# A new front for an attention + MLP kernel: first quads loaded in halves, log sums by scan, one first-layer group parked in SBUF

## The chip, the cores and the metric

One core of one Trainium2 chip runs one program. The metric is the device time of one execution in microseconds. A core has five engines with a queue each, and every engine works through its queue in order: TensorE (PE; its weight loads are shown apart as PEld), VectorE (DVE), ScalarE (ACT), GpSimd (POOL) and SyncE (SP). DMAs are issued from the queues of SP, ACT and POOL and moved by 16 DMA engines that all of them share. A DMA that also casts (fp32 in memory to bf16 on chip) is issued by GpSimd in this kernel.

## What is computed

Attention with a forget gate for 8 batches x 8 heads, 576 tokens, 64 columns a head; its output, 4608 tokens x 512, goes through an MLP of two layers.

```python
scores = scale * np.matmul(q, k.transpose(0, 1, 3, 2))
cum = np.cumsum(np.log(np.clip(f, 0.0001, 1.0)), axis=-1)
decay = cum[:, :, :, None] - cum[:, :, None, :]
scores = np.where(causal, -1000000000.0, scores + decay)
attn = softmax(scores)
x = (attn @ v).transpose(0, 2, 1, 3).reshape(B * S, H * D)   # 4608 x 512
out = gelu_tanh(x @ w_in) @ w_out                            # 512 -> 2048 -> 512
```

The factor exp(-cum) of the decay is put on the values and on the column that sums the denominators, so that a row's own factor drops out: `wT = exp(-cum - 64)`, `vw = v * wT`, and the denominator is a product with `wT` in bf16 (`w_bf`).

## The kernel before

**Units of work.** Four heads make a quad, 16 quads in all, two to a batch. A quad's scores are written in tiles of `[128 keys, 2 heads, up to 512 queries]` in PSUM (pool `psS`, two buffers), and ScalarE's exp takes them to `pt` in SBUF, which frees the buffer (`scores`, L259). Masks are put on `pt` by GpSimd (`mask`, L287) or by VectorE as a product (`mask_by_product`, L311). `denominators` (L356) multiplies `pt` by `w_bf` on TensorE; VectorE transposes the result, takes reciprocals and spreads them (`rb`). `attn_out` (L374) multiplies `pt` by half of `vw`, and VectorE scales by `rb` into `xT`, the input of the MLP, in a ring of four batches. Chunks of 512 tokens then go through the first layer (`mlp_in`, for chunk 0 in halves of 256 tokens by `mlp_in_half`, L408) with ScalarE's Gelu into `gT`, and through the second (`mlp_out`, L658, for chunk 0; `seven_products` later).

**The order** is written by hand. With `manual_schedule` the instructions of each engine stand in the order in which the code issues them, and a table of words sets that order (`run`, L807): each word names an entry of `ops` (L754) with its numbers. In the words of the tables, `LK.i`/`LQ.i` load k/q of quad i with a cast (L206), `TK.i`/`TQ.i` transpose them on VectorE (L212), `S.i.r` or `H.i.r.g` are scores of round r (for all four heads, or for pair g), `M`/`m` masks on GpSimd/VectorE, `VW`/`vw` the product v * wT on GpSimd/VectorE, `CL` a copy of a part of vw, `D` denominators, `V`/`v` attention output, `J.h.g` a first-layer group of 4 x 128 columns for half h of chunk 0 (`j`: the same in the PSUM buffer of pool `psO`, its Gelu issued later by `GJ`), `F.0.n`/`f.0.n` n steps of the second layer of chunk 0, `WI`/`WO` parts of w_in/w_out, `LP`/`LC`/`LV` parts of v, `X` ScalarE's table for exp, and `B.n.c` n products of c columns on zeros that keep TensorE busy. Quads 0 and 1 have four rounds, whose first covers the first 256 queries, so that D and V of them go in two parts (`D.0.0`, `V.0.0.0`).

**The front** is `setup` (L677) and the first rows of `FRONT` (L75) up to `F.0.4`. `setup` loads f by SyncE, and k and q of quads 0 and 1 whole by GpSimd; VectorE clips f, ScalarE takes the log, TensorE transposes it (L700), ScalarE copies it to SBUF (L702, L703). `CW` (`make_w`, L717) then sums along the tokens on TensorE by products with a triangle of ones and with ones, in fp32 (L719, L721), and ScalarE's exp makes `wT` (L724); `W` casts it (L748). Scores of quad 0 (`S.0.0`) stand between. GpSimd's queue has, behind one another, loads, five memsets (`Z`, L705), masks and `VW`. GpSimd's loads use eight semaphores in turn, so a ninth waits for the first to land.

## Time and profile before

| | |
|---|---|
| runs, us | 324.0 (median), 323.05, 324.26 |
| the profiled execution, us | 323.22 |
| its span, us | 321.4 |
| bytes read from and written to HBM | 36.85 and 9.44 MB |
| first scores (L277) start, us from the span's start | 8.62 |
| first first-layer product (L419) | 21.57 |
| first second-layer product of chunk 0 (L667) | 40.82 |
| first first-layer product of chunk 1 (L395) | 66.25 |

The times in the lower rows are from the chain that ended last. The profile is that of one execution; its span leaves out what lies ahead of the first instruction and behind the last, and the difference to the execution's time is 1.8 us. In the profile's lines, `L277` is line 277 of the kernel before; a line reads engine, operation, output<-input, shapes, and then busy time and mean duration, or start and length. TensorE's instructions overlap in its pipeline, so that a mean duration is longer than the distance from one to the next.

### The profile page before, as it was taken

The page shows a single profiled execution, that of the slowest core. Times are in us where ns is not written, and L with a number is a line of the kernel's source. Part 1 is how long each engine was busy: PE and PEld are TensorE (multiplying, and loading weights), DVE is VectorE, ACT ScalarE, POOL GpSimd, SP SyncE. Part 2 cuts the span into 40 slices and gives each one's busy share as a digit, 9 for nine tenths or more (in the row PEclk, how much of TensorE's full clock was granted, in tenths as well). Part 3 has the DMA queues.
Part 4 walks back from the last instruction along what each step waited for, and adds up shares of the span by engine and source line. Part 5 has one row for each costly group of instructions (what it writes and reads, how often), then busy time and mean ns, then how long its engine had stood idle before and what let it go on. Part 6 is the DMA issues. An engine that isn't in the chain of part 4 may idle for free.

```text
span 321.4 us, 11820 instructions
## 1 busy us (share of the span) xinstructions
PE 309.6 (96%) x5339; PEld 220.7 (69%) x5339; DVE 242.0 (75%) x374; ACT 212.7 (66%) x242; POOL 107.8 (34%) x145
## 2 busy tenths in 40 slices
PE   0899999999999999999999999999999999999996
PEld 0557844544776567776788878767776786688785
DVE  4765337898979879779877987699876866597674
ACT  4676576775766776878767866787586744836610
POOL 8989343522301416400851075205610140000000
PEclk9999999999999999999999999999999999999999
DMA  7999999585126931593139411971011111010203
GB/s 126 218 210 208 247 213 199 104 155 109 35 43 129 227 78 37 116 209 72 39 82 228 87 39 35 190 172 36 7 47 53 37 34 37 30 37 0 100 33 99
DMA packets 47490, 33.41 MB, mean 104 GB/s; under 512 B 29776, under 2 KB 42192, under 8 KB 47440
## 3 DMA queue, kind: packets, MB, share of 16 engines
q0 software_dynamic: 9632, 15.99, 28.3%
q1 hardware_dynamic: 37664, 16.60, 19.1%
q8 instruction: 41, 0.67, 0.9%
q14 instruction: 9, 0.07, 0.1%
q10 hardware_dynamic: 144, 0.07, 0.1%
HBM read 36.85 MB, written 9.44 MB: 144 GB/s over the span
## 4 chain that ended last, share of the span: by engine, by line
PE 91%; ACT 3%; DVE 3%; DMA 2%; issue 1%; POOL 0%; DVEq 0%; POOLq 0%
PE ps_w L600 30%; PE ps_h L395 19%; PE ps_s L277 9%; PE po L347 9%; PE ps_q L520 8%; PE pso L667 4%; PE ps_h L419 4%; PE ps_u L468 4%; DMA q_c<-in_q_dram 2%; PE po_m L333 1%; ACT pt L285 1%; ACT gT L403 1%; DVE xT L379 1%; PE idle_ps L256 1%; PE cum_ps L721 1%
## 5 line engine op out<-in xcount | busy, mean ns | idle before, releaser
L285 ACT ACTIVATE pt<-ps_s 128x1024 bf16<-128x1024 f32 (+2 forms) x100 | 94.0, 990 | 38.6 <-PE ps_s L277 35.9
L291 POOL TENSOR_SCALAR_AFFINE_SELECT pt<-pt 128x512 bf16<-128x512 bf16 (+3 forms) x65 | 41.4, 647 | 95.2 <-ACT pt L285 72.3
L395 PE MATMUL ps_h<-xT,w_in_sb 128*128 128x512 bf16 (+1 forms) x320 | 66.8, 358 | 0.3 <-ACT gT L403 0.2
L395 PEld LDWEIGHTS <-w_in_sb 128*128 128x128 bf16 x320 | 31.2, 98 | 26.6 <-issue 0.6
L600 PEld LDWEIGHTS <-gT 128*32 128x32 bf16 (+1 forms) x1216 | 44.1, 97 | 5.5 <-issue 2.2
L403 ACT ACTIVATE gT<-ps_h 128x1024 bf16<-128x1024 f32 x34 | 34.6, 1017 | 18.7 <-PE ps_h L395 18.4
L600 PE MATMUL ps_w<-w_out_sb,gT 128*32 128x256 bf16 (+1 forms) x1008 | 42.6, 273 | 0.0
L277 PE MATMUL ps_s<-qT,kT 32*128 32x64 bf16 (+5 forms) x896 | 36.3, 263 | 3.2 <-DVE qT L214 3.0
L600 PEld LDWEIGHTS <-gsum 128*32 128x32 bf16 (+1 forms) x948 | 35.4, 97 | 3.8 <-issue 1.5
L231 POOL TENSOR_TENSOR vw<-v_nat,wT 128x1280 bf16<-128x1280 f32 (+1 forms) x13 | 29.6, 2279 | 11.7 <-DMA v_nat<-in_v_dram 11.4
L536 DVE TENSOR_TENSOR usnap<-ps_q,usnap 128x1024 f32<-128x1024 f32 x15 | 17.9, 1222 | 18.6 <-PE ps_q L520 13.2
L277 PEld LDWEIGHTS <-kT 32*128 32x128 bf16 x896 | 16.5, 93 | 19.6 <-issue 10.1
L600 PE MATMUL ps_w<-usum,gsum 128*32 128x256 bf16 (+1 forms) x791 | 30.0, 273 | 0.0
L617 DVE COPY snap<-ps_w 128x512 f32<-128x512 f32 x32 | 21.8, 681 | 6.2 <-PE ps_w L600 6.0
L531 ACT ACTIVATE gT<-usnap 128x1024 bf16<-128x1024 f32 x15 | 15.8, 1054 | 12.1 <-DVE usnap L536 11.8
L379 DVE TENSOR_TENSOR xT<-po,rb 128x576 bf16<-128x576 f32 x26 | 19.5, 752 | 5.6 <-PE po L347 5.3
L347 PE MATMUL po<-pt,vw 128*32 128x64 bf16 (+4 forms) x624 | 22.4, 278 | 0.0
L214 DVE STREAM_TRANSPOSE qT<-q_c 128x576 f32<-128x576 f32 x16 | 19.8, 1246 | 1.7 <-DMA q_c<-in_q_dram 1.7
L347 PEld LDWEIGHTS <-vw 128*32 128x32 bf16 x672 | 14.6, 97 | 9.4 <-issue 2.8
L214 DVE STREAM_TRANSPOSE kT<-k_c 128x576 f32<-128x576 f32 x16 | 19.5, 1246 | 1.9 <-DMA k_c<-in_k_dram 1.9
L208 POOL DMA_DIRECT2D k_c<-in_k_dram x16 | 9.1, 568 | 33.6 <-DVE kT L214 18.0
L520 PEld LDWEIGHTS <-w_in_sb 128*128 128x128 bf16 x160 | 15.6, 98 | 2.5 <-issue 0.4
(135 smaller groups left out, 478.5 us busy)
## 6 DMA issues: line engine op xcount, KB each, us to landing
out_dram<-o_st SPq DMA_DIRECT2D x35, 256.0 KB, 2.3
k_c<-in_k_dram POOLq DMA_DIRECT2D x16, 288.0 KB, 5.3
q_c<-in_q_dram POOLq DMA_DIRECT2D x16, 288.0 KB, 6.3
v_nat<-in_v_dram SPq DMA_DIRECT2D x16, 256.0 KB, 5.4
v_nat<-in_v_dram SPq DMA_DIRECT2D x20, 128.0 KB, 5.1
v_nat<-in_v_dram POOLq DMA_DIRECT2D x8, 256.0 KB, 8.1
w_in_sb<-in_moe_w_in_dram POOLq DMA_DIRECT2D x8, 256.0 KB, 7.8
w_out_sb<-in_moe_w_out_dram POOLq DMA_DIRECT2D x4, 512.0 KB, 11.3
```

The lines of the kernel that those rows point to most:

```text
L214: return nc.vector.transpose(out=dst.rearrange("p s c -> p (s c)").bitcast(FP32) .rearrange("p (t a) -> p a t", a=S // 32), in_=src.rearra ...
L231: return eng.tensor_mul(vw[i % 2][:, t0:t1], vb[:, t0:t1, h0:h0 + 4, :], wT[:, i, t0:t1, :].unsqueeze(3).to_broadcast([128, t1 - t0, 4, D]))
L277: nc.tensor.matmul(tiles[h // 2][:, h % 2, c0:c0 + nq], key_columns(i, key, h, c), qq[32 * h:32 * h + 32, q0:q0 + nq, c], start=(c == 0 an ...
L285: nc.scalar.activation(p[:, 2 * g:2 * g + 2, off:off + n], t[:, :, 0:n], AF.Exp, scale=scale)
L291: nc.gpsimd.affine_select(out=x, in_=x, compare_op=ALU.is_ge, fill=0.0, base=0, pattern=pattern, channel_multiplier=-1)
L347: nc.tensor.matmul(po[r0:r0 + w.shape[-1], 448 + q0:448 + q0 + nq], w, p[:, h, col:col + nq], start=(key in (0, "low")), stop=(key in ("lo ...
L379: nc.vector.tensor_mul(xT[:, 2 * u + x, r0 + s0:r0 + s1], po, rbs[i, part])
L395: nc.tensor.matmul(ph[:, j, n * cols:(n + 1) * cols], w_in_sb[:, dt, 128 * ft:128 * ft + 128], xT[:, dt, h0:h0 + cols], start=(dt == 0 and ...
L403: nc.scalar.activation(gelus(c, 2 * pr, 2), ph, AF.Gelu_apprx_tanh)
L520: nc.tensor.matmul(ps[:, k, HC * n:HC * n + HC], w[:, d, 128 * n:128 * n + 128], x[:, d, :], start=(first and n == 0 and d == 0), stop=(d ...
L600: nc.tensor.matmul(ps[c0:c0 + width, n, cols[0]:cols[1]], x[:, j, 128 * n + c0:128 * n + c0 + width], w[:, j, cols[0]:cols[1]], start=(fir ...
L617: copy(kept[name], ps)
```

## The change

Only the front of the table, the functions that it calls and a few words behind it change.

- k and q of quad 0 come in two parts. The first 256 tokens are loaded by SyncE in fp32 into a part of `pt[1]` that is not in use yet, and cast on chip: k by VectorE (`CK`), q by ScalarE (`CA`). The other 320 tokens, and both parts of quad 1, are loaded by GpSimd with the cast; transposes go by part. f is loaded from ScalarE's queue. ScalarE loads one table that has both log and exp.
- The log sums are made by VectorE's scan along the tokens (`SC`) and then transposed by TensorE (`CT`), in place of the copies and the products L719 and L721. `wT` is made for quads 0 and 1 first (`CE.0`), then for the rest (`CE.1`); the cast likewise (`w.0` on ScalarE, `W.1` on VectorE).
- The memsets of `Z` go from GpSimd to VectorE; that of `logfT` is gone.
- The first-layer groups can be issued in parts (`J.h.g.n`). Group J.0.0 is copied raw to SBUF (`RJ`, into a buffer that is free until later), which frees its PSUM buffer for J.0.1; both have their Gelu later.
- `mlp_out` works on two tiles of 128 tokens in turn, a quarter of the depth at a time, so that w_out's last quarter is needed later.
- The table's front is written anew. Fillers are B.1.512 x3 and B.1.256 x2, where they were B.1.384, B.1.512, B.2.512 x2, B.2.256 and B.1.256 x2. The order of loads is another: all of w_in, then w_out's first part, quad 2's k and q, the rest of w_out, and batch 1's v (`LC`) after quad 3's k and q for the most part. Behind the front, `CL.2` and `CL.3` go to ScalarE (`cl`), `vw.2` stands ahead of `TQ.4` on VectorE, `LV.2.0` comes later, and `VW.3` on GpSimd stands behind `LK.6` and ahead of `M.3.2`, where it stood ahead of `LK.4`.

```diff
+    first = pt[1].rearrange("p h n -> p (h n)").bitcast(FP32)
+    first = [first[:, QA * D // 32 * n:QA * D // 32 * (n + 1)] for n in range(2)]
+
+    def load_first(src, eng, n):
+        eng.dma_start(out=first[n], in_=src[0, 0:4, 0:QA].rearrange("h (p a) d -> h p (a d)", p=32))
+
+    def cast_first(dst, eng, n):
+        copy = eng.copy if eng is nc.scalar else eng.tensor_copy
+        copy(dst[0][:, 0:QA // 32, :].rearrange("p a d -> p (a d)"), first[n])
...
+        if part is not None:
+            s0, s1 = parts[part]
+            return nc.gpsimd.dma_start(
+                out=dst[i % 2][:, s0 // 32:s1 // 32, :].rearrange("p a d -> p (a d)"),
+                in_=src[b, h0:h0 + 4, s0:s1].rearrange("h (p a) d -> h p (a d)", p=32))
...
+    def keep_raw(half, g, copy):
+        raw = (u1, u2, u4)[len(raws)].rearrange("p f n -> p (f n)").bitcast(FP32).rearrange("p (b n) -> p b n", n=QA)
+        raws.append(raw)
+        copy(raw, held[half, g][0])
+        held[half, g][0] = raw
...
-        for n in range(CH // 128):
...
+        for pair in range(CH // 256):
+            psos = [psM.tile([128, D_MODEL], FP32, name="pso", tag="m") for _ in range(2)]
+            for part in range(4):
+                for n in range(2):
...
     def setup():
-        nc.sync.dma_start(out=f_sb, in_=f.rearrange("b h s -> (b h) s"))
-        dmas["LK.0"] = load_one(k, k_c, 0)
-        dmas["LQ.0"] = load_one(q, q_c, 0)
+        load_first(k, nc.sync, 0)
+        nc.scalar.dma_start(out=f_sb, in_=f.rearrange("b h s -> (b h) s"))
+        load_first(q, nc.sync, 1)
+        nc.scalar.preload_act_table_set("natural_log_exp_and_others")
+        load_one(k, k_c, 1, 0)
+        load_one(q, q_c, 1, 0)
         make_identity(nc, ident_f32)
-        dmas["LK.1"] = load_one(k, k_c, 1)
-        dmas["LQ.1"] = load_one(q, q_c, 1)
-        make_upper_triangular(nc, utri_f32, val=1.0, diag=True)
...
+        load_one(k, k_c, 0, 1)
+        load_one(q, q_c, 0, 1)
...
+    def running_sums():
+        nc.vector.tensor_tensor_scan(f_sb, ones_f32[0:BH, 0:1].to_broadcast([BH, S]), f_sb, 0.0,
+                                     op0=ALU.mult, op1=ALU.add)
...
-    def make_w():
-        cum_ps = psM.tile([128, NT * BH], FP32, name="cum_ps", tag="m")
-        nc.tensor.matmul(cum_ps, utri_f32, logfT, start=True, stop=True)
-        for n in range(NT - 1, 0, -1):
-            nc.tensor.matmul(cum_ps[:, n * BH:], ones_f32, logfT[:, :(NT - n) * BH], start=False, stop=True,
-                             skip_group_check=True)
+    def cum_tiles():
+        cums.append(psM.tile([128, NT * BH], FP32, name="cum_ps", tag="m"))
+        for t in range(NT):
+            n = min(128, S - 128 * t)
+            nc.tensor.transpose(cums[0][:n, t * BH:(t + 1) * BH], f_sb[:, 128 * t:128 * t + n], ident_f32)
```

The table's front after the change, with line breaks put in:

```
CK TK.0.0 CA TQ.0.0 LK.1.1 LQ.1.1 LP.0 LP.1 S.0.0 SC TK.1.0 TQ.1.0 CT CE.0 w.0 S.1.0 UT CE.1 M.0.0 WI.0 B.1.512
TK.0.1 TQ.0.1 TK.1.1 H.0.1.0 D.0.0 H.0.1.1 B.1.512 WI.1 M.1.0 TQ.1.1 vw.0.0 vw.1.0 H.0.2.0 B.1.512 H.0.2.1 B.1.256
H.1.1.0 V.0.0.0 V.0.1.0 LP.2 LP.3 WI.2 WI.3 H.1.1.1 D.1.0 H.1.2.0 B.1.256 V.1.0.0 H.1.2.1 V.1.1.0 LP.4 WI.4 WI.5 M.0.1
H.0.3.0 j.0.0.8 H.0.3.1 j.0.0.8 WI.6 M.0.3 H.1.3.0 RJ.0.0 vw.0.1 WI.7 D.0.1 j.0.1.8 H.1.3.1 V.0.0.1 V.0.1.1 j.0.1.8
WO.0 M.1.1 M.1.3 VW.1.1 LK.2 LQ.2 WO.1 GJ.0.0 GJ.0.1 WO.2 D.1.1 J.0.2 WO.3 V.1.0.1 V.1.1.1 LC.1.4 W.1 TR J.0.3 LK.3 LQ.3
LC.1.2 LC.1.0 LC.1.1 J.1.0 LC.1.3 J.1.1 TK.2 J.1.2 TQ.2 LQ.4 J.1.3 LK.4 F.0.4 X F.0.4 S.2.0 F.0.11 TK.3 S.2.2 F.0.6 TQ.3
F.0.4 LK.5 S.2.1 F.0.3 F.0.6 vw.2 TQ.4 m.2.1 S.3.0 cl.2 M.2.2 f.0.5 M.2.0 f.0.2 D.2 S.3.1 LV.2.0 f.0.7 LQ.5 V.2.0 m.3.0
S.3.2 TK.4 LK.6 VW.3 f.0.1 f.0.3 V.2.1 M.3.2 f.0.2 S.4.1 cl.3 m.3.1 LQ.6 f.0.5 TQ.5 H.4.2.1 D.3 H.4.0.1
```

More of the change, by code (lines that the diff above doesn't have):

```diff
@@ L414, in mlp_in_half @@
         n0 = QA * half
+        at = [ph.rearrange("p a (b n) -> p (a b) n", n=QA)]
+        later[half, g] = lambda: nc.scalar.activation(gT[:, 4 * g:4 * g + 4, n0:n0 + QA], at[0], AF.Gelu_apprx_tanh)
+        held[half, g] = at
         for dts in (range(N_DT - 1), range(N_DT - 1, N_DT)):
@@ L425, in mlp_in_half @@
                     )
-        later[half, g] = lambda: nc.scalar.activation(gT[:, 4 * g:4 * g + 4, n0:n0 + QA],
-                             ph.rearrange("p a (b n) -> p (a b) n", n=QA), AF.Gelu_apprx_tanh)
-        if not spare:
-            later[half, g]()
+                    if not spare and j == 3 and dt == N_DT - 1:
+                        later[half, g]()
+                    yield
     def x_block(c, b, t):
```

129 lines of the change are left out of this document (63 added, 66 removed).

## Prediction

> **What bounds the kernel now.** I read the page's busy times first, then those by stretch, then the chain that ended last in order of time. Busy us of each engine, with its share of the span of 321.4 us:
>
> ```profile
> PE 309.6 (96%) x5339; PEld 220.7 (69%) x5339; DVE 242.0 (75%) x374; ACT 212.7 (66%) x242; POOL 107.8 (34%) x145
> ```
>
> TensorE (PE) is busy 309.6 of 321.4 us, so 11.8 us at most can come from filling its gaps; more comes only from giving it less work. The view by stretches cuts the span at the first scores (8.62), the first product of the first layer (21.57), the first product of the second layer (40.82) and the first product of chunk 1 (66.25). Behind each stretch stand the busy us of PE, PEld, DVE, ACT and POOL, the clock, the DMA share and GB/s:
>
> ```profile
> 0.00:8.62 8.62, 0.77 (x6) 0.65 (x7) 4.22 (x14) 3.72 (x5) 7.28 (x20) 1.00 0.76 132
> 8.62:21.57 12.95, 12.68 (x165) 6.95 (x165) 9.08 (x18) 10.23 (x14) 12.35 (x18) 1.00 1.12 217
> 21.57:40.82 19.25, 19.08 (x265) 15.48 (x266) 8.19 (x16) 11.38 (x13) 12.03 (x17) 1.00 1.20 226
> 40.82:66.25 25.43, 25.34 (x454) 12.04 (x453) 17.52 (x25) 18.86 (x21) 12.20 (x16) 1.00 0.81 161
> 66.25:321.40 255.15, 251.72 (x4452) 185.56 (x4451) 203.02 (x304) 168.46 (x191) 63.98 (x77) 1.00 0.36 82
> ```
>
> Of the idle 11.8 us, 7.85 lie ahead of the first scores. From 8.62 to 66.25 PE is idle for 0.53 us, and later for 3.4 us in 255. So a shift of the front passes nearly whole to the end, and so does a new wait of PE. The DMA share, over 1 from 8.62 to 40.82, says that the loads run without a gap: they can be put in another order, hardly all moved forward.
>
> The chain in order of time (start, length, what) has the pieces that the change touches:
>
> ```profile
> 2.03 5.25 DMA q_c<-in_q_dram
> 7.28 0.02 issue
> 7.30 1.27 DVE qT L214
> 8.57 0.04 issue
> 8.62 0.83 PE ps_s L277 x14
> 9.45 0.43 PE idle_ps L256
> 9.88 1.07 PE cum_ps L719 x2
> 10.94 1.66 PE cum_ps L721 x8
> ...
> 40.82 1.73 PE pso L667 x8
> ```
>
> **Part 1: the first scores.** They wait for quad 0's q, which lands at 7.28, and for its transpose. New: SyncE loads 256 of the 576 tokens of k, then of q, 256 KB each; VectorE casts k, ScalarE casts q behind its Ln, and VectorE transposes 8/18 of the words. The DMA issues on SyncE's queue, KB each and median us from issue to landing:
>
> ```profile
> out_dram<-o_st SPq DMA_DIRECT2D x35, 256.0 KB, 2.3
> ...
> f_all<-in_f_dram SPq DMA_DIRECT2D x1, 144.0 KB, 2.7
> out_dram<-v_nat SPq DMA_DIRECT2D x1, 128.0 KB, 1.9
> ```
>
> The timeline (start, length): SyncE's first issue,
>
> ```profile
> 0.82 0.58 SPq L678 DMA_DIRECT2D f_all<-in_f_dram  x1
> ```
>
> VectorE's clip of f, with its wait for the load,
>
> ```profile
> 3.58 0.45 DVE L694 TENSOR_SCALAR f_all<-f_all 64x576 f32<-64x576 f32 x1 [1.32 <-DMA f_all<-in_f_dram]
> ```
>
> ScalarE's Ln,
>
> ```profile
> 4.06 0.68 ACT L695 ACTIVATE f_all<-f_all 64x576 f32<-64x576 f32 x1 [1.97 <-DVE f_all L694]
> ```
>
> and PE's five transposes of it:
>
> ```profile
> 4.89 0.77 PE L700 MATMUL ps_lt<-ident_f,f_all 64*128 64x64 f32 x5 [4.89 <-ACT f_all L695]
> ```
>
> The prices of a transpose of 576 words, of a copy of 512 fp32 columns on VectorE and of 256 on ScalarE (busy us, mean ns), each from the groups by shape:
>
> ```profile
> L214 DVE STREAM_TRANSPOSE qT<-q_c 128x576 f32<-128x576 f32 x6 | 7.5, 1248 | 1.7 <-DMA q_c<-in_q_dram 1.7
> ```
>
> ```profile
> L672 DVE COPY o_st<-pso 128x512 f32<-128x512 f32 x3 | 2.0, 678 | 12.1 <-PE pso L667 12.1
> ```
>
> ```profile
> L702 ACT COPY logfT<-ps_lt 128x256 f32<-128x256 f32 x1 | 0.4, 372 | 0.9 <-PE ps_lt L700 0.9
> ```
>
> No row has a 256 KB fp32 load by SyncE at the start. The nearest are a store of that size (2.3 us to landing) and quad 0's q in the chain (5.25, behind k on GpSimd's queue). I take 2.9, near the store and f's 2.7: k, issued at 0.82, lands at 3.7, and q, 0.58 later, at 4.3; the two ends put q at 3.7 to 6.7. f moves to ScalarE's queue and I leave it at 3.58. ScalarE: Ln ends at 4.74, then the cast of 512 columns, about 0.6 (372 ns for 256): 5.35. VectorE: k's cast at most 0.68, each transpose 1248 x 8/18 = 0.55 us, q's done at 5.9. The scores start at about **6.0 in place of 8.62: -2.6 us**. The memsets that VectorE takes over from GpSimd lie in the 1.32 us in which it waits for f; if f lands earlier they show, by up to half a microsecond.
>
> **Part 2: TensorE's work from there to the second layer.** The triangular sums go: 1.07 + 1.66 = 2.73 us. The five transposes that stood ahead of 8.62 (0.77) now stand behind the first scores, since the scan follows q's transpose. The scan has no row: 0.45 (the 576-element clip) to 1.25 (the 576-word transpose) are its ends; I take 1.25, being serial along the row. It costs PE nothing of its own, since S.1.0 behind it waits for two more transposes. Fillers shrink from 3968 to 2048 columns:
>
> ```profile
> L256 PE MATMUL idle_ps<-idle 128*128 128x512 bf16 x5 | 1.4, 383 | 0.0
> ```
>
> ```profile
> L256 PE MATMUL idle_ps<-idle 128*128 128x256 bf16 x4 | 1.0, 280 | 0.0
> ```
>
> ```profile
> L256 PE MATMUL idle_ps<-idle 128*128 128x384 bf16 x1 | 0.5, 499 | 0.0
> ```
>
> From 256 to 512 columns a filler grows by 103 ns, so 1920 columns fewer are 0.77 us. Work from first scores to second layer: 40.82 - 8.62 - 2.73 + 0.77 - 0.77 = **29.5 us instead of 32.2**. The 384-column filler, at 9.4 us, took 499 ns, longer than 512 columns later (383): TensorE was still slow there. [...] I put no term for slow matmuls at the start, because PE waits for ScalarE there anyway (next).
>
> **Part 3: what is late next.** ScalarE's exps of quads 0 and 1:
>
> ```profile
> L285 ACT ACTIVATE pt<-ps_s 128x768 bf16<-128x768 f32 x8 | 6.3, 810 | 3.5 <-PE ps_s L277 3.4
> L285 ACT ACTIVATE pt<-ps_s 128x1024 bf16<-128x1024 f32 x4 | 4.0, 1021 | 0.1
> L285 ACT ACTIVATE pt<-ps_s 128x640 bf16<-128x640 f32 x4 | 2.6, 695 | 0.4 <-PE ps_s L277 0.4
> ```
>
> Each pair of scores needs a PSUM buffer that an exp frees, so PE follows ScalarE here. New: S.0.0's exps from 6.9 to 8.5; cumulative sums' exps and a cast for two quads, about 0.6; S.1.0's scores wait for the transposes behind the scan (8.5) and end at 9.3, exps to 10.9; the remaining sums' exps 0.6; three tiles of H.0 (1.02 + 1.02 + 0.7) to 14.2. From 6.0 to 14.2 PE has about 5.7 us of work (two S groups of 0.83, transposes 0.77, four H tiles, one D, one filler), so it idles 2.5. From there its own work leads, with j.0.0 and j.0.1 filling what ScalarE leaves open. The second layer starts at 6.0 + 29.5 + 2.5 = **38.0 instead of 40.82: -2.8 us**. If ScalarE never holds PE up it is 35.5, and with 4 us of such idling 39.5. Parking J.0.0 costs VectorE a copy of 1024 columns (twice 678 ns) while PE is on H.1.3 and D.0.1, and ScalarE nothing, as its Gelu comes later anyway. j.0.0 needs its two parts of w_in at about 18, 3.6 us before the old first product at 21.57; loads that come late are rival (c).
>
> **Part 4: behind the front.** GpSimd's product of quad 3's vw (VW.3) is moved past LK.6, in front of quad 3's last masks (M.3.2). LK.6 waits for TK.4, which frees its buffer. Timeline rows of before:
>
> ```profile
> 43.76 2.33 POOL L231 TENSOR_TENSOR vw<-v_nat,wT 128x1280 bf16<-128x1280 f32 x1 [6.31 <-DMA v_nat<-in_v_dram]
> ...
> 59.56 0.53 POOL L208 DMA_DIRECT2D k_c<-in_k_dram  x1 [8.42 <-ACT pt L285]
> 60.14 1.40 POOL L291 TENSOR_SCALAR_AFFINE_SELECT pt<-pt 128x512 bf16<-128x512 bf16 x2
> ```
>
> ```profile
> 61.85 0.87 PE L347 MATMUL po<-pt,w_bf 128*32 128x512 bf16 x24
> ```
>
> GpSimd is idle for 8.42 us ahead of LK.6; VW.3 at 2.33 us is not put there but behind it, so M.3.2 ends at 61.54 + 2.33 = 63.87 on the old clock. D.3 on PE (61.85) needs the second of these masks after its first two thirds, at about 62.4: PE waits **1.5 us**. Queued behind D.3 are quad 4's scores and V.3, then chunk 1's first layer. The wait is between 0 (if TK.4 moves forward by that much) and 2.33. vw.2 moved ahead of TQ.4 and m.2.1 on VectorE puts D.2's mask 1.46 us later, about where PE needs it: I count nothing. The paired order of the second layer (mlp_out) issues the same 64 steps and needs w_out's last part later, which covers a later load. CL.2 and CL.3 on ScalarE lie in its gaps.
>
> **Sum:** -2.8 + 1.5 = **-1.3 us**. The profiled execution took 323.22 (span 321.4), the runs 324.0, 323.05 and 324.26; the four average 323.6, so **322.3 us**.
>
> **Rivals.** (a) No wait at D.3, or less idling behind the scores: the full -2.8, 320.8 us. For it: PE idled hardly at all in this stretch before. Against it: M.3.2 stands behind VW.3 on GpSimd's queue.
>
> (b) Slower: the first loads land late. Their source has four heads as its outer dimension, while every load of before has 64, 128 or 256 rows there. If such a load is spread over a quarter of the engines, it takes four times as long to move. From the rows, 128 KB more cost 2.3 - 1.9 = 0.4 us on all engines; 512 KB on a quarter are 6.4 us, and with the 1.5 us that the 128 KB store leaves beside its bytes q lands at 0.82 + 1.5 + 6.4 = 8.7, its cast and transpose end at 9.9: the scores start at 10.0 and not at 6.0, 4.0 us later, so 322.3 + 4.0 = 326.3 us. The sum turns positive where the start slips by over 1.3 us, which is q landing behind 6.1 (6.1 + 0.6 + 0.55 = 7.3). [...]
>
> (c) The change doesn't do what it says: the scores start earlier, but the loads, without a gap as before, still set when the second layer can go on, and the gain is gone by 50 us while D.3's wait stays: 323.6 + 1.5 = 325.1 us. For it: VW.3 waited 6.31 us for batch 1's v, and now v comes behind k and q of quad 3. Against it: in the new order its first reader comes later, too.
>
> **How the numbers follow.** The forecast holds 0.38, (a) 0.22, (b) 0.28, (c) 0.12. The range runs from 319.5 (PE held up by neither) to 327.0 (b with its queue shared). Below 0.5% (1.6 us, what a measurement of this kernel can tell from no change) nothing is told apart. Faster than 322.0: half of the forecast and nearly all of (a), 0.40. Slower than 325.2: (b) and a third of (c), 0.32. Between: 0.28. Because both signs hold chance, the forecast's own range: 320.8 to 323.8.
>
> **What would show it.** The first scores' start (6.0; 10 is rival b) and landing of the two SyncE loads (2.9 us); no L719/L721 rows; the first second-layer product at 38; GpSimd's vw product in front of two masks, PE's wait at D.3 of 1.5 us; the first product of chunk 1 at 65. Wrong would be: idling of PE over 4 us between 6 and 38, or q's landing behind 6.1.

## The result and the profile after

The change makes the kernel **slower**: 340.52 us (median of 340.15, 340.28, 340.76 and 343.38) against 323.86 us for the kernel before in the same rounds, a ratio of **1.054 (1.048 to 1.060)**. The forecast was 322.3 with a range of 319.5 to 327.0: wrong in sign, and outside the range. The profiled execution is the one of 343.38 us (span 341.6), 3 us above the others; its mean granted clock is 0.994 and theirs 0.999 to 1.000, so the fall of the clock at 71 us that is described below is its own. Executions of one kernel differ, in some of the runs below by 5 to 7 us; ratios and intervals leave the most disturbed ones out (one each of e5, e7 and e17, four of e13), the medians do not.

Busy us of each engine, from the page after:

```profile
PE 315.8 (92%) x5308; PEld 220.5 (65%) x5324; DVE 244.7 (72%) x381; ACT 213.3 (62%) x245; POOL 109.0 (32%) x144
```

The program has 15 products fewer than before (the weight loads, 5324 against 5339, show it; another 16 products are missing from the trace), and yet TensorE is busy 6.2 us longer: the same work took longer. Idle time rose from 11.8 to 25.8 us. The view by stretches of the kernel after, cut at the same events (first scores, first layer, second layer, chunk 1); behind each stretch busy us of PE, PEld, DVE, ACT, POOL, the clock, the DMA share, GB/s:

```profile
0.00:15.99 15.99, 0.00 (x0) 0.10 (x1) 4.68 (x18) 2.58 (x3) 7.36 (x16) 1.00 0.80 121
15.99:31.51 15.52, 14.22 (x145) 5.63 (x146) 9.36 (x19) 10.89 (x17) 10.37 (x15) 1.00 0.74 128
31.51:54.88 23.37, 23.37 (x277) 16.78 (x274) 10.40 (x19) 11.61 (x12) 13.77 (x19) 1.00 0.90 136
54.88:86.19 31.31, 27.39 (x455) 12.48 (x454) 16.95 (x23) 19.84 (x23) 13.20 (x17) 0.95 0.83 176
86.19:341.60 255.41, 250.78 (x4439) 185.52 (x4451) 203.34 (x304) 168.40 (x191) 64.27 (x78) 1.00 0.36 82
```

Against before's lengths (8.62, 12.95, 19.25, 25.43, 255.15) each of the four stretches of the front is longer, by 7.4, 2.6, 4.1 and 5.9 us, and the rest by 0.3: 20.2 us, of which 19.9 lie in the front. In the third stretch TensorE is never idle and yet needs 23.37 us for what took 19.25. The causes differ from stretch to stretch.

**First stretch: the first loads.** The chain of work that ended last, after:

```profile
1.60 13.03 DMA pt<-in_q_dram
...
14.65 0.63 ACT q_c L212
...
15.30 0.65 DVE qT L218
```

q's first 256 tokens land 13.03 us after their issue, not 2.9; behind them cast and transpose follow near their prices (0.63 and 0.65 against 0.6 and 0.55), and the scores start at 15.99. GpSimd's six part loads beside them take 11.1 to 13.1 us. The DMA issues after (KB each, median us to landing):

```profile
k_c<-in_k_dram POOLq DMA_DIRECT2D x14, 288.0 KB, 5.1
q_c<-in_q_dram POOLq DMA_DIRECT2D x14, 288.0 KB, 5.6
...
k_c<-in_k_dram POOLq DMA_DIRECT2D x1, 128.0 KB, 13.1
q_c<-in_q_dram POOLq DMA_DIRECT2D x1, 128.0 KB, 12.7
```

Under half the bytes of a whole load (288 KB) take over twice its time. What stands behind them on GpSimd's queue is late with them: v's first two loads, of another form, take 12.0 and 12.2 us.

**Second and third stretch: TensorE's clock.** PE in the timeline after (start, busy us), two steps of eight products of one shape:

```profile
31.51 1.89 PE L434 MATMUL ps_h<-xT,w_in_sb 128*128 128x256 bf16 x8
...
41.52 1.05 PE L434 MATMUL ps_h<-xT,w_in_sb 128*128 128x256 bf16 x8
```

The first is 1.8 times as long as the second. The trace records the first change of the granted clock at 40.31 us, to full; before, it does so at 11.74. Ahead of the first record the clock column shows 1.00 in any case: there the durations tell, not the column. (At 71 us, where the trace does record half clock, products of one shape take 1.7 times as long as just before; see below.)

**Fourth stretch: loads behind masks, and a wait.** GpSimd's queue after, first a row of the timeline, then a piece of the chain:

```profile
18.43 1.22 POOL L295 TENSOR_SCALAR_AFFINE_SELECT pt<-pt 128x512 bf16<-128x512 bf16 x2 [9.80 <-ACT pt L289]
```

```profile
28.18 0.64 POOL w_in_sb L184
28.82 6.22 issue
...
35.08 0.94 POOL pt L295 x2
...
36.03 0.71 POOL w_in_sb L184
36.74 0.77 POOL w_out_sb L188
```

GpSimd waits 9.8 us until ScalarE's exp has written what the first mask (L295) works on, and the first load of w_in stands behind that mask, at 19.6. It waits 6.2 us more for a later mask ("issue" in the chain; the timeline puts it to an exp), and the last load of w_in and the first of w_out stand behind that one. Before, all of w_in was issued by 21.0 us and half of w_out by 23.8 us. The DMA share after, by 2 us:

```profile
16.00:18.00 2.00, 1.59 (x21) 0.97 (x20) 2.00 (x4) 1.14 (x2) 0.00 (x0) 1.00 0.30 67
18.00:20.00 2.00, 1.63 (x17) 0.75 (x18) 1.81 (x4) 1.72 (x6) 1.56 (x3) 1.00 0.08 27
20.00:22.00 2.00, 1.95 (x22) 0.99 (x23) 0.42 (x1) 2.00 (x4) 1.99 (x4) 1.00 0.46 56
```

Before, it was 1.12 and 1.20 on average in the two stretches from 8.6 to 40.8 us. At 40 us 4.9 MB have landed, before 8.1 MB (packets summed in the two traces). So batch 1's v and quads 2 and 3's k and q come late, and D.2 waits. VectorE, then PE, after:

```profile
67.54 1.49 DVE L235 TENSOR_TENSOR vw<-v_nat,wT 128x1280 bf16<-128x1280 f32 x1 [2.78 <-DMA k_c<-in_k_dram]
...
70.04 0.41 DVE L325 TENSOR_TENSOR pt<-pt,causal 128x512 bf16<-128x512 bf16 x1
```

```profile
65.95 1.70 PE L683 MATMUL pso<-w_out_sb,gT 128*32 128x512 bf16 x28
...
70.50 0.61 PE L351 MATMUL po<-pt,w_bf 128*1 128x448 bf16 x16 [2.61 <-DVE pt L325]
...
72.01 2.88 PE L683 MATMUL pso<-w_out_sb,gT 128*32 128x512 bf16 x28
...
81.78 0.31 PE L351 MATMUL po<-pt,w_bf 128*1 128x320 bf16 x4 [0.64 <-POOL pt L295]
82.37 0.28 PE L351 MATMUL po<-pt,w_bf 128*1 128x192 bf16 x8 [0.29 <-POOL pt L295]
```

vw.2 waits for a load until 67.54 (its row names k_c; the part of batch 1's v that it reads is issued at 56.71 and lands at 67.41), the mask m.2.1 stands behind it and a transpose, and PE idles 2.61 us. The clock then falls to half for 3.41 us (71.03 to 74.44), which two groups of 28 products of one shape show: 2.88 us against 1.70. D.3 waits 0.64 and 0.29 us.

### The profile page after: what moved, and what is told of

It reads as the page before. It is cut to its first block, busy times and chain, and to the rows that moved or that the text cites. A ratio compares the mean times of both kernels' runs of the same rounds, so it can differ in the third digit from the quotient of the medians.

```text
span 341.6 us, 11791 instructions
## 1 busy us (share of the span) xinstructions
PE 315.8 (92%) x5308; PEld 220.5 (65%) x5324; DVE 244.7 (72%) x381; ACT 213.3 (62%) x245; POOL 109.0 (32%) x144
## 4 chain that ended last, share of the span: by engine, by line
PE 71%; DMA 9%; issue 8%; POOL 6%; ACT 3%; DVE 2%; SPq 0%; POOLq 0%; DVEq 0%
PE ps_w L614 28%; PE ps_h L399 18%; PE ps_q L534 8%; PE po L351 8%; PE ps_s L281 6%; DMA pt<-in_q_dram 4%; PE ps_u L482 4%; DMA w_out_sb<-in_moe_w_out_dram 4%; POOL pt L295 2%; DMA k_c<-in_k_dram 2%; POOL w_in_sb L184 2%; ACT pt L289 1%; POOL v_nat L172 1%; POOL w_out_sb L188 1%; ACT gT L407 1%
## 5 line engine op out<-in xcount | busy, mean ns | idle before, releaser
L295 POOL TENSOR_SCALAR_AFFINE_SELECT pt<-pt 128x512 bf16<-128x512 bf16 (+3 forms) x67 | 42.1, 639 | 111.7 <-ACT pt L289 88.9
L399 PE MATMUL ps_h<-xT,w_in_sb 128*128 128x512 bf16 (+1 forms) x307 | 65.5, 357 | 1.2 <-ACT gT L407 0.2
L281 PE MATMUL ps_s<-qT,kT 32*128 32x64 bf16 (+5 forms) x896 | 41.0, 278 | 16.9 <-DVE qT L218 16.2
L399 PEld LDWEIGHTS <-w_in_sb 128*128 128x128 bf16 x320 | 31.2, 98 | 26.7 <-issue 0.6
L281 PEld LDWEIGHTS <-kT 32*128 32x128 bf16 x896 | 17.5, 96 | 35.0 <-issue 18.9
L550 DVE TENSOR_TENSOR usnap<-ps_q,usnap 128x1024 f32<-128x1024 f32 x15 | 17.9, 1221 | 18.6 <-PE ps_q L534 13.2
L614 PE MATMUL ps_w<-usum,gsum 128*32 128x256 bf16 (+1 forms) x791 | 29.8, 273 | 0.0
L218 DVE STREAM_TRANSPOSE kT<-k_c 128x576 f32<-128x576 f32 (+2 forms) x18 | 19.7, 1120 | 9.2 <-DMA k_c<-in_k_dram 9.1
L218 DVE STREAM_TRANSPOSE qT<-q_c 128x576 f32<-128x576 f32 (+2 forms) x18 | 20.0, 1118 | 7.7 <-ACT q_c L212 7.2
L545 ACT ACTIVATE gT<-usnap 128x1024 bf16<-128x1024 f32 x15 | 15.8, 1054 | 12.1 <-DVE usnap L550 11.8
L351 PEld LDWEIGHTS <-vw 128*32 128x32 bf16 x672 | 14.6, 97 | 9.6 <-issue 3.1
L200 POOL DMA_DIRECT2D k_c<-in_k_dram x14 | 7.9, 561 | 36.7 <-DVE kT L218 36.7
L434 PE MATMUL ps_h<-xT,w_in_sb 128*128 128x256 bf16 x128 | 17.5, 300 | 0.0
```

Source lines behind the costliest of these rows:

```text
L218: return nc.vector.transpose(out=dst[:, s0:s1].rearrange("p s c -> p (s c)").bitcast(FP32) .rearrange("p (t a) -> p a t", a=n), in_=src[:, ...
L281: nc.tensor.matmul(tiles[h // 2][:, h % 2, c0:c0 + nq], key_columns(i, key, h, c), qq[32 * h:32 * h + 32, q0:q0 + nq, c], start=(c == 0 an ...
L295: nc.gpsimd.affine_select(out=x, in_=x, compare_op=ALU.is_ge, fill=0.0, base=0, pattern=pattern, channel_multiplier=-1)
L351: nc.tensor.matmul(po[r0:r0 + w.shape[-1], 448 + q0:448 + q0 + nq], w, p[:, h, col:col + nq], start=(key in (0, "low")), stop=(key in ("lo ...
L399: nc.tensor.matmul(ph[:, j, n * cols:(n + 1) * cols], w_in_sb[:, dt, 128 * ft:128 * ft + 128], xT[:, dt, h0:h0 + cols], start=(dt == 0 and ...
L614: nc.tensor.matmul(ps[c0:c0 + width, n, cols[0]:cols[1]], x[:, j, 128 * n + c0:128 * n + c0 + width], w[:, j, cols[0]:cols[1]], start=(fir ...
```

## The experiments

Three theories stood after the first profile, and the question was the share of each. **Loads**: four heads as outermost dimension make the first loads late. **Clock**: the fp32 products and fillers taken out were what brought TensorE to full clock. **Order**: words of the table, loads behind masks or vw.2 and VW.3, make the front wait. The table gives all runs: median time in us, ratio with its interval (each against the kernel before on the same chip, 323.7 to 324.1 us), and from the profiled execution the start of the stages (as the timeline has them; the chain puts before's first and second layer at 21.57 and 40.82) and the time at which the trace first records full clock.

| run | us | ratio | first scores | first layer | second layer | chunk 1 | full clock |
|---|---|---|---|---|---|---|---|
| before | 323.9 | | 8.62 | 21.50 | 40.66 | 66.25 | 11.7 |
| the change | 340.5 | 1.054 (1.048-1.060) | 15.99 | 31.51 | 54.88 | 86.19 | 40.3 |
| e1_whole_loads | 335.3 | 1.036 (1.033-1.038) | 8.52 | 25.18 | 46.89 | 76.35 | none recorded |
| e2_first_by_head | 338.3 | 1.044 (1.041-1.047) | 12.04 | 28.59 | 49.91 | 81.39 | 32.1 |
| e3_parts_alone | 332.3 | 1.026 (1.024-1.028) | 9.73 | 28.22 | 49.53 | 75.12 | 15.8, half 19.2-32.9 |
| e4_more_fillers | 335.6 | 1.037 (1.035-1.039) | 16.32 | 30.29 | 50.01 | 79.00 | 21.3 |
| e5_whole_fillers | 333.1 | 1.027 (1.024-1.030) | 8.30 | 29.36 | 51.43 | 80.52 | 35.3 |
| e6_whole_order | 336.9 | 1.040 (1.039-1.042) | 8.92 | 25.60 | 47.29 | 79.64 | 29.9 |
| e7_whole_fillers_order | 334.0 | 1.029 (1.025-1.033) | 8.60 | 25.81 | 45.53 | 79.55 | 20.3 |
| e8_before_scan_thin | 328.6 | 1.015 (1.013-1.016) | 8.59 | 24.83 | 46.13 | 71.72 | 29.5 |
| e9_whole_loads_early | 331.1 | 1.023 (1.020-1.026) | 8.36 | 25.68 | 47.06 | 74.00 | 29.4 |
| e10_change_loads_early | 338.3 | 1.045 (1.041-1.049) | 15.11 | 31.00 | 54.38 | 81.33 | 39.9 |
| e11_whole_all | 328.9 | 1.015 (1.010-1.020) | 8.38 | 26.13 | 45.85 | 72.04 | 21.2 |
| e12_before_scan | 329.4 | 1.017 (1.015-1.020) | 8.44 | 25.83 | 46.96 | 72.55 | 30.1 |
| e13_before_warm | 326.0 | 1.001 (0.998-1.005) | 8.79 | 21.38 | 40.52 | 66.13 | 10.1 |
| e14_before_scan_warm | 330.5 | 1.019 (1.017-1.021) | 9.84 | 26.52 | 47.52 | 73.11 | 6.6, half 10.0-30.5 |
| e15_whole_all_warm | 326.0 | 1.007 (1.004-1.011) | 8.90 | 22.52 | 42.24 | 69.13 | 5.1 |
| e16_whole_loads_warm | 331.2 | 1.023 (1.020-1.026) | 8.69 | 25.43 | 47.13 | 73.32 | 5.9, half 12.7-29.8 |
| e17_whole_all_warm_trim | 332.1 | 1.021 (1.017-1.026) | 8.90 | 24.45 | 44.17 | 70.36 | 6.0, half 12.8-19.7 |
| e18_change_warm | 334.8 | 1.033 (1.030-1.037) | 16.25 | 28.34 | 48.62 | 76.86 | 6.9 |

The profiled execution is the longest of e5 (337.5) and of e7 (337.1) and the shortest of e17 (327.5). Falls to half clock behind the start of the second layer, which the last column leaves out, stand in the traces of the change (71.0 to 74.4), e2 (66.3 to 69.7), e6 (60.6 to 64.0) and e7 (57.8 to 64.7).

### The loads: e1, e2, e3

e1 takes the four loads of the start whole from GpSimd and transposes them whole; all else is the change.

```diff
-        load_first(k, nc.sync, 0)
-        load_first(q, nc.sync, 1)
-        load_one(k, k_c, 1, 0)
...
+        load_one(k, k_c, 0)
+        load_one(q, q_c, 0)
```

Expected: 

> The changed kernel with k and q of quads 0 and 1 loaded whole by GpSimd, as before (128 rows of memory as the outer dimension), and transposed whole; all else stays changed. Theory A, the loads whose source has four heads outermost are spread over four engines and that is the loss: q of quad 0 lands at about 7.3 us, the first scores start at about 8.7, and the time is 321 to 327 us. Theory B, the rest of the new front (order, scan, GpSimd's queue) costs most: 333 us or more with the first scores at 8.7.

Measured 335.3, in theory B's range: the scores start at 8.52, but 11.6 of the 16.7 us stay. The late start is worth 5.2 us, and there are other causes.

e2 splits the two SyncE loads by head, so that no load of quad 0's first tokens has four heads outermost (q goes by ScalarE's queue, quad 1 whole; LK.0.1 and LQ.0.1 stay as they are).

```diff
-        eng.dma_start(out=first[n], in_=src[0, 0:4, 0:QA].rearrange("h (p a) d -> h p (a d)", p=32))
+        for h in range(4):
+            eng.dma_start(out=first[n][32 * h:32 * h + 32, :], in_=src[0, h, 0:QA].rearrange("(p a) d -> p (a d)", p=32))
```

Expected: 

> The changed kernel with the first 256 tokens of quad 0 loaded by one DMA per head (32 rows outermost), k on SyncE's queue and q on ScalarE's, and quad 1 loaded whole; the other 320 tokens of quad 0 stay as two loads with four heads outermost. Theory A: the fp32 loads land within 5 us of their issue instead of 13, the two loads left with four heads outermost still take 8 us or more, first scores at 6 to 9 us, 320 to 328 us. Rival, fp32 loads from a hardware queue are slow beside GpSimd's loads whatever their shape: q lands at 10 us or later, 330 us or more.

Measured 338.3, first scores at 12.04. Its chain:

```profile
3.84 6.83 DMA pt<-in_q_dram
```

That is only the last of q's four heads, issued fourth on ScalarE's queue; it lands at 10.68. The four take 2.9 to 6.8 us each, against 13.03 for the one load of the change. k by head is complete at 8.1, later than the one load of the change (6.7). So theory A **missed** (landing within 5 us, scores from 6 to 9, 320 to 328 us), and the figures that came in are the rival's (q at 10 or later, 330 or more). The run doesn't tell form from queue: q also changed its queue, four loads stand behind one another where there was one, and quad 1 came whole.

e3 puts only the part loads of quads 0 and 1 into the kernel before, all by GpSimd.

```diff
-        dmas["LK.0"] = load_one(k, k_c, 0)
-        dmas["LQ.0"] = load_one(q, q_c, 0)
+        load_one(k, k_c, 0, 0)
+        load_one(q, q_c, 0, 0)
```

Expected: 

> The kernel before with one part of the change alone: k and q of quads 0 and 1 loaded in two parts each by GpSimd, four heads outermost, and transposed by part. Theory A: these eight loads land 10 us or more after their issue, where whole ones took 4.6 to 7.4, and the time rises to 328 to 336 us. Rival, only the pair of hardware loads is slow: landing within 8 us and a time within 1% of before.

Measured 332.3, 8.5 us slower than before, though the scores start only 1.1 us later. The time is in theory A's range, the landing isn't: the eight loads take 5.8 to 9.4 us, where before's four whole ones take 4.6 to 7.4. e3's chain and its stretch up to the first layer say why:

```profile
2.21 6.81 DMA q_c<-in_q_dram
...
9.31 8.80 DMA v_nat<-in_v_dram
```

```profile
9.73:28.22 18.49, 17.53 (x164) 7.95 (x164) 10.62 (x24) 10.76 (x14) 16.18 (x27) 0.76 1.18 205
```

v lands behind the slow loads, at 18.1, TensorE is held up, and its mean granted clock in the stretch is 0.76: here a late load costs its wait, and the clock on top. The packets of GpSimd's queue (packets, MB, share), before and in e3:

```profile
q0 software_dynamic: 9632, 15.99, 28.3%
```

```profile
q0 software_dynamic: 13280, 16.01, 29.5%
```

Eight part loads bring 3648 packets more for the same bytes.

### The clock: e4, e8, e12, e13, e14

e4 gives the change larger fillers (B.n.512) between the scores.

```diff
- S.0.0 SC TK.1.0 ... WI.0 B.1.512 ... H.0.1.1 B.1.512 ... H.0.2.0 B.1.512 H.0.2.1 B.1.256
+ S.0.0 SC B.4.512 TK.1.0 ... WI.0 B.4.512 ... H.0.1.1 B.4.512 ... H.0.2.0 B.3.512 H.0.2.1 B.3.512
```

Expected: 

> The changed kernel with more products on zeros between the first scores and the first-layer groups: 18 of 512 columns where there were 3 of 512 and 1 of 256. Theory A1, TensorE runs at half clock from 16 to 40 us because it idles in between, and that costs several us: the full clock comes by 25 us and the time falls by 2 to 6 us against 340.5. Rival A2, the late loads set the end of this stretch and the clock costs nothing: 339 to 342 us.

Measured 335.6, 5.0 us faster than the change, as theory A1 says, by adding work that computes nothing.

e8 goes the other way: the kernel before with the scan and with the change's 2048 filler columns.

```diff
+        nc.vector.tensor_tensor_scan(f_sb, ones_f32[0:BH, 0:1].to_broadcast([BH, S]), f_sb, 0.0, op0=ALU.mult, op1=ALU.add)
...
- S.0.0 B.1.384 CW ... LP.3 B.1.512 vw.0.0 B.2.512 ... WI.2 B.2.512
+ S.0.0 CW ... LP.3 B.1.512 vw.0.0 B.1.512 ... WI.2 B.1.512
```

Expected: 

> The kernel before with the log sums by scan in place of the fp32 products, and with the 2048 filler columns of the change in place of 3968; loads and order untouched. As the prediction priced it: TensorE has 2.7 us less of products and 0.8 us less of fillers to do, 320.5 to 322.5 us. Clock theory: the products and fillers removed are what brought TensorE to full clock at 11.7 us; without them it stays at half clock past 16 us and loses more than it saves, the second layer at 42 to 46: 325 to 330 us.

e12 is the same with all of before's fillers:

Expected: 

> The kernel before with the log sums by scan in place of the fp32 products, all of its fillers kept (e8_before_scan_thin with the fillers back). If it was the thinned fillers that cost the clock in e8: full clock by 14 us and 2 us less of products, 321.5 to 323.5 us. If it was the missing fp32 products: the clock stays at half past 16 us as in e8, 326 to 329 us.

Measured 328.6 (in the clock theory's range) and 329.4 (0.4 above the range for missing fp32 products), 4.8 and 5.6 us slower than before, with before's loads and order; e12 with all fillers is no better than e8, so it is the fp32 products: **taking 2.7 us of them out costs 5.6 us**. e12 in stretches of 3.41 us up to the change of the clock at 30.14, first PE whole (its busy us, clock, DMA share, GB/s), then the first layer's products alone (PE, ACT, clock):

```profile
16.49:19.90 3.41, 3.41 (x46) 1.00 1.17 197
19.90:23.32 3.42, 3.42 (x36) 1.00 1.18 203
23.32:26.73 3.41, 3.41 (x38) 1.00 1.15 177
26.73:30.14 3.41, 3.41 (x25) 1.00 1.17 221
```

```profile
16.49:19.90 3.41, 0.00 (x0) 0.00 (x0) 1.00 1.17 197
19.90:23.32 3.42, 0.00 (x0) 0.00 (x0) 1.00 1.18 203
23.32:26.73 3.41, 0.90 (x5) 0.00 (x0) 1.00 1.15 177
26.73:30.14 3.41, 2.69 (x13) 0.00 (x0) 1.00 1.17 221
```

and before, ahead of its change at 11.74, whole and the fp32 sums alone:

```profile
8.32:11.74 3.42, 3.12 (x24) 2.38 (x24) 1.79 (x5) 1.51 (x2) 3.42 (x5) 1.00 1.07 245
```

```profile
8.32:11.74 3.42, 2.07 (x7) 1.96 (x8) 0.00 (x0) 1.00 1.07 245
```

In e12 TensorE is busy without a gap in all four stretches. Behind the first three the clock stays at half; it is full only behind the fourth, which is filled mostly by products of the whole array (128 rows by 128 columns: first layer, fp32 sums, fillers). Scores (32 rows) and attention output (32 columns), which fill most of the first three, don't do it. Ahead of the change of the clock 16 first-layer products take 3.59 us (from 25.83 on), behind it 32 of them take 3.67 (from 33.47 on). The length of 3.41 us comes from the traces: the changes of the clock that they record lie that far apart, or a whole multiple of it, at 40.31, 71.03 and 74.44 us in the change (nine times 3.41, then once) and at 6.59, 10.00 and 30.48 in e14 (once, then six times). To be busy for such a stretch was not enough, as e12's first three rows show.

e13 puts 14 fillers ahead of before's first scores, and e14 puts 17 ahead of e12's.

```diff
         nc.vector.memset(idle, 0.0)
+        keep_busy(7)
...
-        TK.0 LP.0 LP.1
+        B.7.512 TK.0 LP.0 LP.1
```

Expected: 

> The kernel before with 14 products of 512 columns on zeros ahead of its first scores, where TensorE is idle from 0 to 8.62 us; nothing else. Clock theory: TensorE comes to full clock before 8.6 instead of at 11.74, and the scores and fp32 products between 8.62 and 11.74 take half as long: 0.5 to 2 us less, 322 to 323.3. Rival (from 8.62 to 21.5 VectorE, ScalarE or the loads set the pace as soon as TensorE is faster): no difference over 0.5 us.

Expected: 

> e12_before_scan (329.4 us) with 17 such products ahead of the first scores. Clock theory: all of the scan's loss is the half clock until 30 us, so with a clock that is full at 8.6 the scan is worth what the prediction said, and the time is 321 to 323.5 us. Rival (the scan itself costs, by VectorE's order: the first scores or quad 1's k come later): 326 to 329 us.

e13 doesn't decide. By its ratio the earlier clock brings nothing, and the second layer of the profiled execution starts at 40.52 against 40.66, as the rival has it. But of its twelve executions the five fastest, at a mean granted clock of 0.999 or more, take 322.6 to 323.3 us, which is the clock theory's range (before, in the same rounds: 323.2 to 324.8). A sixth takes 325.0, two take 327.1 at 0.984 and four 328.5 to 328.8 at 0.979: where the clock falls back, about 5 us are gone. e14 **missed** both expectations. It has the clock, and loses it again; three stretches of e14, with the clock as the third number from the end:

```profile
3.18:6.59 3.41, 3.41 (x9) 1.21 (x8) 2.24 (x3) 1.97 (x2) 3.30 (x7) 1.00 1.05 166
6.59:10.00 3.41, 1.29 (x13) 0.54 (x15) 2.14 (x5) 0.00 (x0) 3.35 (x8) 1.00 1.00 170
10.00:30.48 20.48, 20.07 (x180) 8.74 (x175) 9.70 (x20) 11.50 (x15) 12.63 (x19) 0.50 1.12 200
```

From 10.00 to 30.48 PE is busy 20.07 of 20.48 us at a recorded 0.50, and the first and second layer start at 26.52 and 47.52, about as late as in e12 (25.83 and 46.96): e12's lengths are those of a half clock.

### The order: e5, e6, e7, e9, e10, e11

All but e10 build on e1. e5 adds e4's fillers; e6 puts words back as before (batch 1's v ahead of quad 3's k and q, VW.3 ahead of LK.4, vw.2 behind m.2.1); e7 has both.

```diff
- LK.3 LQ.3 LC.1.2 LC.1.0 LC.1.1 J.1.0 LC.1.3 J.1.1 ... LQ.4 J.1.3 LK.4 ... vw.2 TQ.4 m.2.1 S.3.0 ... LK.6 VW.3
+ LC.1.2 LC.1.0 LC.1.1 LC.1.3 LK.3 J.1.0 LQ.3 J.1.1 ... LQ.4 VW.3 J.1.3 LK.4 ... TQ.4 m.2.1 S.3.0 vw.2 ... LK.6
```

Expected: 

> The whole loads of e1_whole_loads (335.3 us, scores from 8.52, second layer from 46.9) with the four larger groups of fillers of e4_more_fillers. Clock theory: what was left of the late second layer in e1_whole_loads was TensorE at half clock from 8.5 to about 29 us. With fillers the clock is full before 15 us and the second layer starts at 41 to 43: 330 to 332 us. Rival (the loads in their new order bind the front): the second layer stays behind 45, 334 to 336 us.

Expected: 

> e1_whole_loads with the words behind the front as in the kernel before: batch 1's v ahead of quad 3's k and q, the GpSimd product VW.3 ahead of LK.4, vw.2 behind m.2.1 and S.3.0 on VectorE. Order theory: the waits of TensorE at D.2 (2.6 us, and 3.4 us at half clock behind it) and at D.3 (0.9) go, chunk 1 starts 3.5 to 5 us earlier: 330.5 to 332 us. Rival (the v loads only take the place of k and q, which are late in their turn): less than 1 us, 334.5 to 336 us.

Expected: 

> Both edits, e5's fillers and e6's order, on the whole loads. If the two causes are separate, their gains add: 335.3 - 4 - 4 = 327 us (326 to 328.5). Rival (one cause, the clock: with a full clock D.2 waits no longer, or waits longer because TensorE comes earlier): no better than the better one of the two by more than 1 us, 329.5 to 331.

e5 came out at 333.1, 1 us above its expectation and below its rival's, but its profiled execution reached full clock only at 35.3 us; it doesn't decide. e6 and e7 **missed**: 336.9 and 334.0. With the v loads ahead, quad 3's q is issued at 48.57 behind waits for w_out's DMAs, and PE waits 4.76 us for what stands behind its transpose on VectorE (POOL, then PE, of e6):

```profile
48.57 0.55 POOL L200 DMA_DIRECT2D q_c<-in_q_dram  x1 [2.01 <-DMA w_out_sb<-in_moe_w_out_dram]
```

```profile
61.19 2.72 PE L683 MATMUL pso<-w_out_sb,gT 128*128 128x512 bf16 x6 [4.76 <-DVE o_st L689]
```

So D.2 no longer waits, and another product waits longer. All loads of this part are late, and an exchange of words only picks which is last. (That it is not the place of vw.2 that makes D.2 wait, as my order theory had it, is seen in e10 below.)

e9 (on e1) and e10 (on the change) therefore move the loads ahead of the masks and change nothing else; e11 has whole loads, fillers, e6's words and the early loads.

```diff
- LP.0 LP.1 S.0.0 ... CE.1 M.0.0 WI.0 ... WI.1 M.1.0 ... V.0.1.0 LP.2 LP.3 WI.2 WI.3 ... WI.6 M.0.3 ... WO.0 M.1.1
+ LP.0 LP.1 WI.0 WI.1 S.0.0 ... CE.1 LP.2 LP.3 LP.4 WI.2 M.0.0 WI.3 ... WI.4 WI.5 M.1.0 WI.6 LQ.2 WI.7 ... V.0.1.0 LK.2 LC.1.4 WO.0 WO.1 ... M.0.3 ... M.1.1
```

Expected: 

> e1_whole_loads (335.3 us; second layer from 46.9) with the GpSimd words for w_in, v, quad 2's k and q and w_out's first half moved ahead of the masks behind which the change put them, to about where the kernel before has them; nothing else. Load theory: the masks wait for ScalarE's exp, so loads behind them leave the DMA queues empty (in e1_whole_loads 4.4 MB have landed at 30 us, in the kernel before 5.7); issued early they land at before's rate and the second layer starts at 42 to 44: 328 to 331 us. Clock theory (TensorE's half clock until 29 us sets the front, e8_before_scan_thin with before's loads lost 4.8 us by it): less than 2 us, 333.5 to 335.5.

Expected: 

> The change itself (340.5 us) with the same words moved, and the loads with four heads outermost kept. Load theory: the gap in the DMA share from 16 to 21 us is filled, and the second layer starts 3 to 6 us earlier: 335 to 338 us. Rival (the slow first loads hold the queues, and what is issued earlier lands no earlier): within 1.5 us of the change, 339 to 342; first scores may even come later than 16.0.

Expected: 

> All four edits together: whole loads, more fillers, batch 1's v and the vw products as before, and the loads ahead of the masks. If these are the causes, what is left of the change is the scan, the parked group, the paired second layer and the table order, and the time is within 1 per cent of the kernel before: 321 to 327 us, second layer from 40 to 42. If a cause is still unnamed: 328 or more.

e9: 331.1, as the load theory said, but by another way than it said: first and second layer start as late as in e1, and the gain is behind them, 26.9 us to chunk 1 in place of 29.5, since D.2 no longer waits. e10 likewise: 338.3, with the second layer at 54.38 and not 3 to 6 us earlier, and from the second layer to chunk 1

```profile
54.38:81.33 26.95, 25.88 (x456) 12.11 (x454) 17.09 (x23) 19.83 (x23) 11.20 (x14) 1.00 0.74 155
```

in place of 31.31 (which has the fall of the clock that the change's other executions don't have), with vw.2 where the change has it. D.3 still waits 0.63 and 0.29 us there: that wait is VW.3's. e11: 328.9, so a cause was left; in it the clock is full only from 21.2 us.

### The rest: e15, e16, e17, e18

e15 is e11 with 18 fillers ahead of the first scores, e16 the same without e4's fillers, e17 with two thirds of them, and e18 is e4 with 52 fillers ahead of its scores.

```diff
+        nc.vector.memset(idle, 0.0)
+        keep_busy(18)
         nc.vector.memset(ones_f32, 1.0)
```

Expected: 

> e11_whole_all (328.9 us, full clock from 21.2) with 18 such products ahead of the first scores. If the half clock from 8.4 to 21.2 us is what is left of the loss: second layer from 40 to 42, 322.5 to 325 us. If another cause is left (the order of the words, loads): 326.5 to 329.

Expected: 

> e15_whole_all_warm without the larger fillers between the scores (the change's own fillers of 512 and 256 columns). If a clock once full stays full: 1 to 2 us better than e15, 321 to 324 us, since the fillers cost TensorE time. If thin work lets the clock fall back to half: worse than e15, 327 us or more.

Expected: 

> e15_whole_all_warm (325.95 us) with 12 instead of 18 products of 512 columns in its five groups of fillers between the scores. If the clock stays full with these: about 1.2 us of TensorE work less (six at 0.21), 323.5 to 325, level with the kernel before. If it falls back to half as in e16: 328 to 331.

Expected: 

> e4_more_fillers (the change with larger fillers, 335.55 us, full clock from 21.3) with 52 products of 512 columns ahead of its first scores at 16 us: the change with the clock out of the way, its late loads and its order kept. If the clock from 16 to 21 us is worth what e15 got against e11: 2 to 3 us less, 332.5 to 334. If the loads, issued behind masks, set the front by then: within 1 us of e4, 334.5 to 336.5.

e15: 326.0, between its two expectations, 3.0 us better than e11, second layer at 42.24; all but 2.1 of the 16.7 us are back. (Two of its five executions, both 328.1 at a mean clock of 0.990, fell back.) e16: 331.2, the second of its expectations: thin work lets the clock fall to half from 12.7 to 29.8 us. e17: 332.1, above both, fallen back as well, so what the fillers themselves cost was not measured. e18: 334.8, within 1 us of e4, as the second of its expectations says (loads behind masks); the stretches that follow its scores,

```profile
16.25:28.34 12.09, 11.72 (x159) 5.00 (x160) 9.15 (x19) 10.42 (x17) 9.93 (x15) 1.00 0.65 116
28.34:48.62 20.28, 20.14 (x276) 15.49 (x273) 10.16 (x20) 11.70 (x13) 14.60 (x20) 1.00 1.18 189
```

are 12.09 and 20.28 long, near before's 12.95 and 19.25 (the change's: 15.52 and 23.37). With the clock cured, the second stretch is cured and the third all but 1.0 us, and the late start and the late loads stay.

**The account**, each cause undone alone in the change: whole loads -5.2 us (e1), the clock -5.8 (e18), the loads ahead of masks -2.2 (e10), 13.2 in all; with e6's words beside them, everything together -14.6 (e15). The remaining 2.1 us is not settled. e15 has 9472 filler columns between its scores, where before has 3968, but that is not what shows. Two stretches of e15 and one wait in the first of them:

```profile
8.90:22.52 13.62, 11.72 (x159) 5.00 (x160) 8.74 (x15) 10.42 (x17) 10.55 (x16) 1.00 1.16 216
42.24:69.13 26.89, 25.81 (x454) 12.04 (x454) 17.05 (x23) 19.67 (x23) 12.54 (x16) 1.00 0.87 164
```

```profile
12.57 0.52 PE L281 MATMUL ps_s<-qT,kT 32*128 32x256 bf16 x16 [1.74 <-DVE qT L218]
```

Between first scores and first layer PE is busy 11.72 us, less than in the kernel before (12.6), and idle for 1.9, of which 1.74 are a wait for quad 1's q, whose transpose stands behind the scan on VectorE. From the second layer to chunk 1 it is idle for 1.1 us, where before it was for 0.1. No run undoes these waits. By median no version beat the kernel before.

## Why the prediction was wrong, point by point

**Part 1, the first scores: wrong, the first failed step.** "SyncE loads 256 of the 576 tokens" at 2.9 us each, q landing at 4.3: k landed 5.9 us after its issue, q 13.0, at 14.6 and so far behind the 6.1 that I had named as a sign of being wrong. I took a load's time from its bytes, from rows of loads with 64 to 256 rows outermost, and used it for one with four. Rival (b) had the direction. Its quarter of the engines (6.4 us for 512 KB) was an assumption of mine, and no run shows on how many engines a load ran. What the packet records show in its place: the two SyncE loads together leave 8 packets of 4 bytes, f's load alone 16. From 4 to 6 us SyncE's queue has 4.2 packets in flight on average, where GpSimd's queue in the kernel before, with whole loads, has 16.7 from 3 to 9. The rival's price was too low (10.0 against 15.99). It took the two loads for alone; GpSimd's six part loads of the same form, 11.1 to 13.1 us each, lie beside them, and from 7 to 12 us, when only q's load is left on SyncE's queue, 2.4 packets of it are in flight. With whole loads the scores start at 8.52 (e1); how much of the 13.0 is the form of the load and how much the neighbours, no run separates.

**Part 2, PE's work: wrong, the second failed step.** The 2.73 us of fp32 products did go, and the fillers were halved. "I put no term for slow matmuls at the start, because PE waits for ScalarE there anyway" was the error: PE was busy without a gap from 23 us on, at half clock, until 40.3. From first scores to second layer it took 38.9 us, where 29.5 of work and 2.5 of idling were forecast. I priced the removed work by its time and not by what it did to the clock: in e12, with the scan alone changed, the kernel is 5.6 us slower.

**Part 3, idling behind ScalarE: of little weight.** PE idled 1.3 us between the first scores and the first layer, in place of 2.5 up to the second; the second layer started at 54.88, not at 38.0. That the loads "run without a gap" and could only be put in another order was true before and false after: I didn't look at what stands behind the masks on GpSimd's queue, where the change put w_in and w_out. That is a sort of rival (c), with 2.2 us (e10), but what it costs shows behind the second layer's start.

**Part 4: the mechanism at D.3 right, its size off.** VW.3 ahead of M.3.2 makes PE wait 0.93 us (1.5 forecast, bounds 0 to 2.33); with the word back, in e15, the wait is gone. **D.2 "I count nothing" was wrong:** PE waited 2.61 us and ran 3.41 us at half clock behind it (the latter in the profiled execution alone), not for vw.2's length but for a late load ahead of it.

The sum's frame held: a shift of the front passes nearly whole to the end (19.9 us ahead of the last stretch, 0.3 in it). The shared error of the range: each rival was priced alone, while the change had a late start, a half clock and late loads at once, worth 5.2, 5.8 and 2.2 us when each is undone alone.

## What to carry to other kernels

Before you take products out of a thin stage, ask what holds TensorE's clock: look for the same shape at two durations, and count work on the whole array, not busy time; here taking out 2.7 us of fp32 products cost 5.6 us, and three stretches of 3.41 busy us left the clock of e12 at half. Read the outermost dimension of a load before its bytes: 128 and 160 KB with four heads outermost took 5.8 to 9.4 us in e3, where 288 KB with 128 rows outermost took 4.6 to 7.4 before. And follow a moved load on its issuing queue: behind a mask that waited 9.8 us for compute, it left the DMA engines a share of 0.08 from 18 to 20 us.
